# Loads, splits and sums of x placed sooner, one weight sum placed inside the first block pair, and q's raw weights issued ahead of the last transpose

## The chip, the cores and the metric

The kernel runs on one core of one Trainium2 chip. The core has a matrix engine (PE, TensorE), which writes its results to the PSUM memory, three engines for element-wise work (DVE or VectorE, ACT or ScalarE, POOL or GpSimd) and a queue engine (SP) that issues most DMA transfers. Each engine works through its own instructions strictly in order and waits at each one for the semaphores that this instruction needs. The metric is the device time of one execution in microseconds (us), as the median of several runs.

## The reference

One input x (2048 rows of 512) goes through two mixers, and a sigmoid gate blends them:

```python
x = A_x
g = _sigmoid((x * gate_w).sum(-1, keepdims=True))
a = _A_ref(x, A_wqkv, A_w_phi, A_wo)
b = _B_ref(x, B_w_q, B_k1, B_k2, B_u, B_v)
return g * a + (1 - g) * b
```

`_A_ref` is linear attention with 32 heads of 16: q, k and v are projections of x; q and k go through a small matrix per head and then a pair of softmaxes, softmax(p) and softmax(-p); `kv` is the sum over all rows of phi_k times v, and the output is phi_q times kv over a normalising sum, times `wo`. `_B_ref` picks for each row and head one of 16 x 16 experts by two maxima over scores (x times `w_q` times the keys `k1`, `k2`), and adds up rows of `v` weighted by a gelu of x times `u`.

## The kernel before

**Blocks.** x is worked on in 16 blocks of 128 rows. The first phase (up to about 157 us) builds what has to be there before any output row: k and v of all 16 blocks and their sum kv, and the folded score weights. The main stage after it computes one output block after the other.

**Three-product matmuls.** Every float32 operand is split into a high part (names ending in h, a copy rounded to the fp32r type) and a low part (ending in l, the difference to the original). A product is then three matmuls, high x high, high x low and low x high (`mm3`, L56 to L58, and `prod`, L446). So each block of x needs a load (`x_load`, L149, SP), a high copy `xh` (`x_high`, L152, on ACT from block 3 on) and a low part `xl` (`x_low`, L156, on DVE). The loaded blocks share four buffers `xr`.

**Blocks 0 to 4** are done singly, in the loop over t. A block has its projections `vproj` and `kproj` on PE, `k_diffs` on DVE (two reductions L115 and L117 and two subtractions L119 and L121: the differences to maximum and minimum, for the two softmaxes), `k_exp` on ACT (L266), `k_sum` on DVE (L270 and the reciprocal L271), `k_mult` on POOL (L275), and later `kvacc` on PE (L282), which adds phi_k times v to kv.

**Blocks 5 to 14** are done in five pairs, t = 5, 7, 9, 11, 13, by a scheme that saves products: seven half-size products instead of eight, with sums of the pair's two blocks (`Sums.add`, four POOL additions in place on the two `xr` buffers, L175 to L178; then `Sums.high` gives `gh` and a second high part on ACT, L183, and `Sums.low` gives `gl` and a second low part on POOL, L188) and with sums of the weights (t1, t2, e and t4, each in a high and a low part; t2h and t2l lie in `uh` and `ul`, and the fourth, t4h and t4l, in a part of `sh` and `sl`). The partial results a, b, c and d (banks named pk, pu, pv, pk) build upon each other: ACT copies a to b (L474), b to c (L483) and b to d (L502) between the products. In the order of PE a pair is: pk (6 matmuls), pe (6), pu (6), pk (6), two score sums `ws`, kvacc, pu (6), pv (6), pk (6).

**Score weights.** The raw weights `w_q` come in 16 pieces of 1 MB (`load_wq`, two buffers `st`, also used for wv, wk and q's raw weights `rawq`). `score` (L298) folds one piece into the bank `ws`. After each second piece `score_planes` (L303, L305) splits the result into two planes of 16 bits on ACT and transposes them by a DMA on SP; `score_join` puts the planes together again (L310, ACT), makes the high part `sh` (L314, ACT) and the low part `sl` (L315, POOL). The planes `wpl`, the transposed planes `wtp` and the joined `wtj` have one buffer each, so the eight rounds follow one another. A new `load_wq` is issued as soon as a score piece has been used.

**The end of the phase.** After the last pair come block 15 alone, the fold of q's weights (`fold_q`, L207, needs `rawq`), the first rows of the scores `front_s(0, 0)` and `front_s(0, 1)` (banks s; the second needs all of joins 4 to 7), the remaining kvacc, and `front_q(0)` (bank pq).

**What sets the order.** The schedule is manual: each engine's instructions stand in the order in which the Python code calls them. Moving a call moves its instruction on every engine that it uses. SP's queue is in order too, so that a load whose buffer is not yet free holds up all that stand behind it.

Of the kernel before, what the change touches and what calls it, by code (L numbers as in the profile page):

```python
# [9 lines left out]
F32 = mybir.dt.float32  # L10
# [6 lines left out]
ALU = mybir.AluOpType  # L17
# [3 lines left out]
P = 128  # L21
S = 2048
D = 512
NT = S // P
# [11 lines left out]
def mix_kernel(ctx, tc, xT, wqT, wkT, wv, wphi, wo, wq, kk, ug, ev, cst, out):  # L36
    nc = tc.nc
    pe, dve, act, pool, sp = nc.tensor, nc.vector, nc.scalar, nc.gpsimd, nc.sync
# [4 lines left out]
    def mm_bank(name):  # L43
        return psum.tile([P, 512], F32, tag="mm", bufs=4, name=name)

    def tr_bank(name):
        return psum.tile([P, 512], F32, tag="tr", bufs=3, name=name)
# [44 lines left out]
    t1h = per.tile([P, 2, D], F32R, name="t1h")  # L92
    t1l = per.tile([P, 2, D], F32R, name="t1l")
# [39 lines left out]
    wa_ = ca.enter_context(tc_pool("wl", "left"))  # L133
# [6 lines left out]
    def stage(src, name, shape=None):  # L140
        t_ = wa_.tile(shape or [P, NK, D], F32, tag="st", bufs=2, name=name)
        if src is not None:
            sp.dma_start(t_, src)
        return t_

    def x_load(t):
        r = rawx[t] = wa_.tile([P, NK, P], F32, tag="xr", bufs=4, name=f"xr{t}")
        if t > 0:
            sp.dma_start(r, xT[t])  # L149

    def x_high(t, ks=slice(0, NK)):
        (dve.tensor_copy if t < 3 else act.copy)(x_of(t)[0][:, ks], rawx[t][:, ks])  # L152

    def x_low(t, ks=slice(0, NK)):
        h, l = x_of(t)
        dve.tensor_tensor(l[:, ks], rawx[t][:, ks], h[:, ks], op=ALU.subtract)  # L156

    def x_split(t, ks=slice(0, NK)):
        x_high(t, ks)
        x_low(t, ks)  # L160

    kraw, t12 = (m.rearrange("p (k d) -> p k d", k=NK) for m in raw4)
    t1r, t2r = t12[:, 0:2], t12[:, 2:4]
    twos = lambda a: a.rearrange("p k n -> p (k n)")[:, :1024].rearrange("p (k n) -> p k n", k=2)
    t2h, t2l = twos(uh), twos(ul)
    t4h, t4l = sh[:, :, 768:1024], sl[:, :, 768:1024]
# [73 lines left out]
    phis, vs, pks, wsP, stk, joins = {}, {}, {}, {}, {}, []  # L240
# [20 lines left out]
    def kproj(t):  # L261
        pks[t] = mm_bank(f"pk{t}")
        proj(pks[t], t, wah, wal, 0, D)

    def k_exp(t):
        act.activation(phis[t], phis[t], AF.Exp)  # L266

    def k_sum(t):
        d, st = phis[t], stk[t]
        dve.tensor_reduce(st[:, 64:128], g64(d), axis=AX.X, op=ALU.add)  # L270
        dve.reciprocal(st[:, 128:192], st[:, 64:128])  # L271

    def k_mult(t):
        d, st = phis[t], stk.pop(t)
        pool.tensor_tensor(g64(d), g64(d), b64(st[:, 128:192]), op=ALU.mult)  # L275
# [17 lines left out]
    def score_w(i, raw):  # L293
        j, par = i // 2, i % 2
        if par == 0:
            wsP[j] = tr_bank(f"ws{j}")
        for c in range(4):
            pe.matmul(wsP[j][32 * c:32 * c + 32, :], kp[:, j // 4, par, :], raw[:, c, :],  # L298
                      start=(par == 0), stop=(par == 1))
# [7 lines left out]

    def score_join(j, tp):
        tj = wa_.tile([P, D], F32, tag="wtj", bufs=1, name=f"wtj{j}")
        act.copy(tj.bitcast(U16).rearrange("p (k n j) -> p j k n", j=2, n=P),  # L310
                 tp.rearrange("p (j k) n -> p j k n", j=2))
        js = slice(P * j, P * j + P)
        t3 = tj.rearrange("p (k e) -> p k e", k=NK)
        act.copy(sh[:, :, js], t3)  # L314
        pool.tensor_tensor(sl[:, :, js], t3, sh[:, :, js], op=ALU.subtract)  # L315
# [22 lines left out]
    x_load(1)  # L338
    rawk = stage(wkT, "rawk")
    x_load(2)  # L340
    wps = mm_bank("warm")
    for _ in range(16):
        pe.matmul(wps[:, :384], warm[:, 1:P + 1], warm[:, :384], start=True, stop=True)
# [27 lines left out]
    def load_wq():  # L371
        if len(raws) < 16:
            raws.append(stage(wq[len(raws)], f"wq{len(raws)}"))

    load_wq()
    load_wq()
    pool.tensor_copy(wm, cs[:, 128:160].rearrange("p (a b) -> p a b", b=F))

    pool.tensor_tensor(t1r, t1r, kraw[:, 0:2], op=ALU.subtract)
    pool.tensor_tensor(t2r, t2r, kraw[:, 0:2], op=ALU.add)  # L380
    act.copy(t1h, t1r)
    pool.tensor_tensor(t1l, t1r, t1h, op=ALU.subtract)

    def spare(src, name, shape):
        t_ = wa_.tile(shape, F32, tag="xr", bufs=4, name=name)
# [5 lines left out]
    def score(n):  # L391
        nonlocal done
        for _ in range(n):
            score_w(done, raws[done])
            done += 1
            load_wq()
            if done % 2 == 0:
                score_planes(done // 2 - 1)

    def join_all():  # L400
        old = list(joins)
        joins.clear()
        for j, tp in old:
            score_join(j, tp)

    plan = {0: 2, 2: 1, 3: 1, 4: 2}
    for t in range(5):
        x_load(t + 3)
        if t > 2:
            vproj(t)()  # L410
        kproj(t)
        k_diffs(t)
        score_old = list(joins)
        joins.clear()
        score(plan.get(t, 0))
        if t % 2 == 0:
            for u in (t - 3, t - 2):
                if u >= 0:
                    kvacc(u)
        if t > 0:  # L420
            x_split(t + 2)
        k_exp(t)
        k_sum(t)
        if t == 0:
            act.copy(t2h, t2r)
            pool.tensor_tensor(t2l, t2r, t2h, op=ALU.subtract)
        k_mult(t)
        if t == 2:
            t4r = kraw[:, 2:4]
            pool.tensor_tensor(t4r, t4r, t2r, op=ALU.subtract)  # L430
            by4 = lambda a: a.rearrange("p k (c n) -> p (k c) n", c=2)
            act.copy(t4h, by4(t4r))
        for j, tp in score_old:
            score_join(j, tp)
    x_load(8)
    Sums.add(5)
    Sums.high(5)
    Sums.low(5)
    pool.tensor_tensor(t4l, by4(t4r), t4h, op=ALU.subtract)
    x_high(7)  # L440
    x_high(8)

    def prod(o, left, right, first):
        for i, ((ah, al), (bh, bl)) in enumerate(zip(left, right)):
            for j, (x_, w_) in enumerate(((ah, bh), (ah, bl), (al, bh))):
                pe.matmul(o, x_, w_, start=(first and i + j == 0), stop=(i == 1 and j == 2),  # L446
                          skip_group_check=True)
# [8 lines left out]
    for t in range(5, NT - 1, 2):  # L456
        n = t + 1
        more = [u for u in (t + 4, t + 5) if u < NT]
        for u in more:
            x_load(u)  # L460
        if t == NT - 5:
            rawu = [spare(ug[:, 0:2], "rawu0", [P, 2, NU])]
        elif t == NT - 3:
            rawu.append(spare(ug[:, 2:4], "rawu1", [P, 2, NU]))
            rawe = [spare(ev[:, 0], "rawe0", [P, D])]
        for u in (t + 2, t + 3):
            if u < NT - 1:
                x_low(u)
        if behind:
            k_diffs(behind)  # L470
        a = pks[t] = mm_bank(f"pk{t}")
        prod(a, tile_of(t, 0), b11, True)
        b = mm_bank(f"pu{t}")
        act.copy(b, a)  # L474
        if t + 3 < NT:
            Sums.add(t + 2)
        if t < NT - 3:
            join_all()
        e = tr_bank(f"pe{t}")
        prod(e, sums(0, 2), b1, True)  # L480
        prod(b, sums(1, 0), b2, False)
        c = mm_bank(f"pv{t}")
        act.copy(c, b)  # L483
        prod(a, tile_of(t, 2), b21, False)
        k_diffs(t)
        if behind:
            k_exp(behind)
            k_sum(behind)
            k_mult(behind)
        score(2)  # L490
        if t == NT - 3:
            rawq = stage(wqT, "rawq")
        for u in (t - 3, t - 2):
            if u > 2:
                kvacc(u)
        k_exp(t)
        k_sum(t)
        vn, vt = v_tile(n), v_tile(t)
        act.copy(vn, by16(e))
        prod(b, sums(0, 0), b3, False)  # L500
        d = pks[n] = mm_bank(f"pk{n}")
        act.copy(d, b)  # L502
        prod(c, sums(1, 2), b22, False)
        dve.tensor_tensor(vt, by16(c), vn, op=ALU.add)
        dve.tensor_tensor(vn, by16(b), vn, op=ALU.add)
        o2 = d.rearrange("p (c n) -> p c n", c=2)
        prod(o2, tile_of(n, 2), b4, False)
        if t + 3 < NT:
            Sums.high(t + 2)
            Sums.low(t + 2)  # L510
        if t == 7:
            for i in range(2):
                x_parts(i, 11)
        for u in more if n < NT - 4 else ():
            x_high(u)
        k_mult(t)
        behind = n
    t = NT - 1
    x_split(t)
    rawe.append(spare(ev[:, 1], "rawe1", [P, D]))  # L520
    k_diffs(t - 1)
    kproj(t)
    k_exp(t - 1)
    k_sum(t - 1)
    for k in range(NK):
        act.copy(uh[:, k, :NU], rawu[k // 2][:, k % 2, :])
        pool.tensor_tensor(ul[:, k, :NU], rawu[k // 2][:, k % 2, :], uh[:, k, :NU], op=ALU.subtract)
    k_mult(t - 1)
    k_diffs(t)
    join_all()  # L530
# [357 lines left out]
    for a in range(NT - 1):  # L888
        n, b, z = a + 1, a - 1, a - 2
# [74 lines left out]
    a, b, z = NT - 1, NT - 2, NT - 3  # L964
# [123 lines left out]
```

## Time and profile before

| | |
|---|---|
| median of 3 runs | 408.52 us (408.52 to 409.42) |
| time of the profiled execution | 410.26 us |
| its span | 407.8 us |
| mean granted TensorE clock | 0.958 |
| busy, share of the span | PE 92%, DVE 81%, ACT 62%, POOL 50% |
| chain that ended last, by engine | PE 73%, DVE 9%, ACT 7%, POOL 4% |
| DMA | 46.67 MB, mean 114 GB/s |

A timeline row gives the start, the length, the engine, the line, the operation with out<-in, the shapes and the count, and in brackets how long the engine was idle before it and which instruction ended that. "PEq" and "SPq" are the queues' own instructions, such as a DMA that is issued. A row of a window gives busy time of PE, PEld, DVE, ACT and POOL, then the granted clock of TensorE (1.00 is full speed), the share of the DMA engines and GB/s. PE's matmuls overlap, so one that is listed with 0.39 us starts 0.23 us after the one before it at full clock.

### The profile page before, as it was taken

The numbers are of one execution on the slowest core, as the hardware profiler recorded it, in microseconds if no ns is written. First come the engines' busy times: TensorE is split into PE (matmuls) and PEld (weight loads), VectorE is DVE, ScalarE is ACT, GpSimd is POOL, SyncE is SP. The second block draws the span as 40 slices with busy tenths as digits, with TensorE's granted clock in tenths as the row PEclk, the third lists the DMA queues.
The fourth block names the chain that finished last, engine by engine and source line by source line (L and its number), as shares of the span: only waits on it lengthen the run. The fifth ranks groups of instructions, "written<-read, shape, count | busy, mean of one in ns | idle before, by whom it ended". The sixth has DMA issues, their size and how long they took to land.

```text
span 407.8 us, 8985 instructions
## 1 busy us (share of the span) xinstructions
PE 375.5 (92%) x3519; PEld 294.2 (72%) x3519; DVE 331.9 (81%) x782; ACT 253.1 (62%) x449; POOL 202.4 (50%) x206
## 2 busy tenths in 40 slices
PE   8998909999998099989999999999999999999996
PEld 4756605776776088868878888888888888888775
DVE  4679536898969409687999999999999999999993
ACT  4564544677743603558769669668677877877731
POOL 1095469777963621448326335444543633554700
PEclk9998966999999669998999999999999999999999
DMA  7755582989670501133542344235145135324111
GB/s 277 260 217 196 166 248 61 276 220 268 132 237 2 155 2 32 50 78 92 79 91 73 72 90 92 66 80 104 26 105 116 39 80 116 61 71 105 39 54 51
DMA packets 72218, 46.67 MB, mean 114 GB/s; under 512 B 63600, under 2 KB 64496, under 8 KB 69872
## 3 DMA queue, kind: packets, MB, share of 16 engines
q1 hardware_dynamic: 71312, 45.24, 42.2%
q10 hardware_dynamic: 864, 0.87, 0.8%
q8 instruction: 27, 0.44, 0.5%
q14 instruction: 15, 0.12, 0.1%
HBM read 26.43 MB, written 4.19 MB: 75 GB/s over the span
## 4 chain that ended last, share of the span: by engine, by line
PE 73%; DVE 9%; ACT 7%; POOL 4%; issue 3%; DMA 3%; SPq 0%; ACTq 0%; POOLq 0%; DVEq 0%
PE po L817 10%; PE s L56 8%; PE s L57 7%; PE s L58 7%; PE po L824 5%; PE pq L56 4%; PE pq L58 4%; PE pq L57 4%; PE pk L446 3%; PE oT L708 2%; PE pu L446 2%; DVE xl L156 2%; PE pp L57 2%; PE pp L58 2%; PE pp L56 2%
## 5 line engine op out<-in xcount | busy, mean ns | idle before, releaser
L622 POOL TENSOR_TENSOR w<-d,zb 128x512 f32<-128x512 f32 x32 | 40.9, 1294 | 83.5 <-ACT d L616 83.5
L56 PE MATMUL s<-sh,xh 128*128 128x512 f32 x128 | 52.3, 408 | 0.0
L57 PE MATMUL s<-sl,xh 128*128 128x512 f32 x128 | 51.1, 399 | 0.0
L58 PE MATMUL s<-sh,xl 128*128 128x512 f32 x128 | 51.0, 398 | 0.0
L275 POOL TENSOR_TENSOR d<-d,st 128x1024 f32<-128x1024 f32 x16 | 32.3, 2020 | 37.2 <-DVE st L271 25.2
L657 POOL TENSOR_TENSOR d<-d,st 128x512 f32<-128x512 f32 x30 | 31.2, 1062 | 28.5 <-DVE st L651 25.6
L616 ACT ACTIVATE d<-d 128x512 f32<-128x512 f32 x32 | 20.1, 632 | 39.8 <-DVE d L119 31.1
L699 ACT COPY pt<-tp 128x1024 uint16<-128x1024 uint16 x28 | 36.4, 1370 | 0.0
L156 DVE TENSOR_TENSOR xl<-xr,xh 128x512 fp32r<-128x512 f32 (+2 forms) x17 | 23.2, 1380 | 12.4 <-ACT xh L152 12.3
L689 ACT COPY pl<-d 128x1024 uint16<-128x1024 uint16 x28 | 29.2, 1045 | 4.3 <-POOL d L657 4.3
L58 PEld LDWEIGHTS s<-sh,xl 128*128 128x128 f32 x128 | 24.7, 193 | 5.3
L56 PEld LDWEIGHTS s<-sh,xh 128*128 128x128 f32 x128 | 24.8, 194 | 5.0
L57 PEld LDWEIGHTS s<-sl,xh 128*128 128x128 f32 x128 | 24.8, 194 | 4.8
L56 PE MATMUL pq<-wah,xh 128*128 128x512 f32 x64 | 26.8, 418 | 0.0
L626 DVE TENSOR_REDUCE st<-d 128x32 f32<-128x512 f32 x32 | 21.7, 682 | 5.4 <-ACT d L616 3.8
L58 PE MATMUL pq<-wah,xl 128*128 128x512 f32 x64 | 25.1, 392 | 0.0
L57 PE MATMUL pq<-wal,xh 128*128 128x512 f32 x64 | 25.0, 390 | 0.0
L266 ACT ACTIVATE d<-d 128x1024 f32<-128x1024 f32 x16 | 17.0, 1062 | 12.2 <-DVE d L121 12.2
L270 DVE TENSOR_REDUCE st<-d 128x64 f32<-128x1024 f32 x16 | 19.3, 1205 | 6.4 <-ACT d L266 6.3
L817 PE MATMUL po<-wbh,xh 128*128 128x512 f32 x60 | 24.0, 400 | 0.0
L817 PE MATMUL po<-wbl,xh 128*128 128x512 f32 x60 | 23.4, 390 | 0.0
L666 DVE TENSOR_TENSOR eq<-s,mx 128x512 bf16<-128x512 f32 x32 | 22.1, 692 | 1.2
(240 smaller groups left out, 1113.6 us busy)
## 6 DMA issues: line engine op xcount, KB each, us to landing
wq<-wq SPq DMA_DIRECT2D x16, 1024.0 KB, 6.0
xr<-xT SPq DMA_DIRECT2D x15, 256.0 KB, 4.7
y<-ot SPq DMA_DIRECT2D x15, 256.0 KB, 2.5
rawk<-wkT SPq DMA_DIRECT2D x1, 1024.0 KB, 6.7
rawq<-wqT SPq DMA_DIRECT2D x1, 1024.0 KB, 4.9
rawo<-wo SPq DMA_DIRECT2D x4, 256.0 KB, 3.6
rawu<-ug SPq DMA_DIRECT2D x2, 258.0 KB, 3.5
rawv<-wv ACTq DMA_DIRECT2D x2, 256.0 KB, 4.7
```

Of the source, the lines that this page charges most:

```text
L56: pe.matmul(o, ah, bh, start=(first and i == 0), stop=False)
L57: pe.matmul(o, ah, bl, start=False, stop=False)
L58: pe.matmul(o, al, bh, start=False, stop=(last and i == n - 1))
L156: dve.tensor_tensor(l[:, ks], rawx[t][:, ks], h[:, ks], op=ALU.subtract)
L275: pool.tensor_tensor(g64(d), g64(d), b64(st[:, 128:192]), op=ALU.mult)
L622: pool.tensor_tensor(hs(e["w"], i), hs(e["ph"], i), hs(zb, i), op=ALU.mult)
L626: dve.tensor_reduce(pair(e["st"][:, 64:128])[:, :, i], hs(e["ph"], i), axis=AX.X, op=ALU.add)
L657: eng.tensor_tensor(g64(d)[:, gs_], g64(d)[:, gs_], r[:, gs_].unsqueeze(2).to_broadcast([P, 32, F]), op=ALU.mult)
L666: dve.tensor_tensor(e["eq"][:, 512 * half:512 * half + 512].rearrange("p (h f) -> p h f", f=F), p3, mx.unsqueeze(2).to_broadcast([P, H, F] ...
L689: act.copy(pl, e["ph"][:, halves[i]].bitcast(U16).rearrange("p (c j) -> p j c", j=2))
L699: act.copy(p16[:, :, 4 * i:4 * i + 4, :], e["tp"][i].rearrange("p (j g) n -> p j g n", j=2))
L817: pe.matmul(po, a, b, start=(i == 0), stop=False)
```

## The change

It moves calls and changes no arithmetic:

- x3 is loaded before the warm-up, x4 to x6 before the first block, x7 and x8 in blocks 1 and 2; before, block t loaded x(t + 3), and x8 came after the loop. Splits go one block ahead: block t < 3 splits x(t + 3), and block 2 also x6.
- The first sums (`Sums.add(5)`, high, low) go from behind the loop into blocks 2 and 3.
- The low part t1l goes into block 0, the difference t4r from block 2 to block 3, and its parts t4h and t4l into pair 5. `k_mult(4)` goes into pair 5, behind t4l.
- The first joins come in blocks 2 and 4 (before: 1 and 4), each before that block's score sum.
- `score_join` is cut in two, `join_tp` (the copy that empties `wtp`) and `join_end`. In pair 13 the seventh join's first half is done; its second half follows behind the pair.
- In pair 13 `rawq` is issued between the two score sums, and x15 is split inside the pair. Behind the pair the parts of u come ahead of `k_exp(14)`.

```diff
@@ score_join
     def score_join(j, tp):
         tj = wa_.tile([P, D], F32, tag="wtj", bufs=1, name=f"wtj{j}")
+        join_tp(j, tp, tj)
+        join_end(j, tj)
+
+    def join_tp(j, tp, tj):
         act.copy(tj.bitcast(U16).rearrange("p (k n j) -> p j k n", j=2, n=P),
                  tp.rearrange("p (j k) n -> p j k n", j=2))
+
+    def join_end(j, tj):
         js = slice(P * j, P * j + P)
         t3 = tj.rearrange("p (k e) -> p k e", k=NK)
         act.copy(sh[:, :, js], t3)
...
     x_load(2)
+    x_load(3)
...
     load_wq()
     load_wq()
+    for t in (4, 5, 6):
+        x_load(t)
...
     act.copy(t1h, t1r)
-    pool.tensor_tensor(t1l, t1r, t1h, op=ALU.subtract)
...
-    plan = {0: 2, 2: 1, 3: 1, 4: 2}
+    t4r = kraw[:, 2:4]
+    by4 = lambda a: a.rearrange("p k (c n) -> p (k c) n", c=2)
     for t in range(5):
-        x_load(t + 3)
+        if t in (1, 2):
+            x_load(t + 6)
         if t > 2:
             vproj(t)()
         kproj(t)
         k_diffs(t)
-        score_old = list(joins)
-        joins.clear()
-        score(plan.get(t, 0))
+        if t in (2, 4):
+            join_all()
+        score((2, 0, 1, 1, 2)[t])
         if t % 2 == 0:
             for u in (t - 3, t - 2):
                 if u >= 0:
                     kvacc(u)
-        if t > 0:
-            x_split(t + 2)
+        if t < 3:
+            x_split(t + 3)
+        if t == 2:
+            x_split(6)
+            Sums.add(5)
+        if t == 3:
+            Sums.high(5)
+            Sums.low(5)
         k_exp(t)
         k_sum(t)
         if t == 0:
             act.copy(t2h, t2r)
+            pool.tensor_tensor(t1l, t1r, t1h, op=ALU.subtract)
+        if t < 4:
+            k_mult(t)
+        if t == 0:
             pool.tensor_tensor(t2l, t2r, t2h, op=ALU.subtract)
-        k_mult(t)
-        if t == 2:
-            t4r = kraw[:, 2:4]
+        if t == 3:
             pool.tensor_tensor(t4r, t4r, t2r, op=ALU.subtract)
-            by4 = lambda a: a.rearrange("p k (c n) -> p (k c) n", c=2)
-            act.copy(t4h, by4(t4r))
-        for j, tp in score_old:
-            score_join(j, tp)
-    x_load(8)
-    Sums.add(5)
-    Sums.high(5)
-    Sums.low(5)
-    pool.tensor_tensor(t4l, by4(t4r), t4h, op=ALU.subtract)
     x_high(7)
     x_high(8)
...
+        if t == 5:
+            act.copy(t4h, by4(t4r))
         if t < NT - 3:
             join_all()
+        else:
+            (j6, tp), = joins
+            joins.clear()
+            tj6 = wa_.tile([P, D], F32, tag="wtj", bufs=1, name="wtj6")
+            join_tp(j6, tp, tj6)
+        if t == 5:
+            pool.tensor_tensor(t4l, by4(t4r), t4h, op=ALU.subtract)
+            k_mult(4)
...
-        score(2)
+        score(1)
         if t == NT - 3:
             rawq = stage(wqT, "rawq")
+        score(1)
...
         prod(c, sums(1, 2), b22, False)
+        if t == NT - 3:
+            x_split(NT - 1)
         dve.tensor_tensor(vt, by16(c), vn, op=ALU.add)
...
     t = NT - 1
-    x_split(t)
     rawe.append(spare(ev[:, 1], "rawe1", [P, D]))
     k_diffs(t - 1)
     kproj(t)
-    k_exp(t - 1)
-    k_sum(t - 1)
+    join_end(j6, tj6)
     for k in range(NK):
         act.copy(uh[:, k, :NU], rawu[k // 2][:, k % 2, :])
         pool.tensor_tensor(ul[:, k, :NU], rawu[k // 2][:, k % 2, :], uh[:, k, :NU], op=ALU.subtract)
+    k_exp(t - 1)
+    k_sum(t - 1)
     k_mult(t - 1)
```

POOL from the end of block 2 to the first sums, before (L275 is `k_mult`, L430 the difference t4r, L245 sets a column of v, L315 a join's low part, L175 to L178 the adds):

```order
L275 TENSOR_TENSOR d_374<-d_374,st_375 128x1024
L430 TENSOR_TENSOR xraw_66<-xraw_66,xraw_69 128x1024
L245 MEMSET v_442 128x32
L275 TENSOR_TENSOR d_458<-d_458,st_459 128x1024
L245 MEMSET v_495 128x32
L275 TENSOR_TENSOR d_511<-d_511,st_512 128x1024
L315 TENSOR_TENSOR sl<-wtj_604,sh 128x4x128
L175 TENSOR_TENSOR xr_427<-xr_427 128x256
L176 TENSOR_TENSOR xr_427<-xr_359,xr_427 128x256
L177 TENSOR_TENSOR xr_359<-xr_427,xr_359 128x256
L178 TENSOR_TENSOR xr_359<-xr_359 128x256
L188 TENSOR_TENSOR gl<-xr_427,gh 128x512
```

And now, from the second `k_mult` (L321 is the join's low part, L448 the difference t4r):

```order
L275 TENSOR_TENSOR d_351<-d_351,st_352 128x1024
L321 TENSOR_TENSOR sl<-wtj_384,sh 128x4x128
L175 TENSOR_TENSOR xr_285<-xr_285 128x256
L176 TENSOR_TENSOR xr_285<-xr_283,xr_285 128x256
L177 TENSOR_TENSOR xr_283<-xr_285,xr_283 128x256
L178 TENSOR_TENSOR xr_283<-xr_283 128x256
L275 TENSOR_TENSOR d_378<-d_378,st_379 128x1024
L245 MEMSET v_452 128x32
L188 TENSOR_TENSOR gl<-xr_285,gh 128x512
L188 TENSOR_TENSOR xl_70<-xr_283,xh_67 128x512
L275 TENSOR_TENSOR d_468<-d_468,st_469 128x1024
L448 TENSOR_TENSOR xraw_66<-xraw_66,xraw_69 128x1024
```

The adds stood behind five `k_mult`; now they stand behind two, and `gl` behind three.

ACT in pair 5, between the copies to b and c, before (L474 and L483 are these copies, L310 and L314 the third join):

```order
L152 CAST xh_65<-xr_608 128x512
L474 COPY pu_634<-pk_627 128x512
L310 COPY wtj_640<-wtp_532 128x2x512
L314 CAST sh<-wtj_640 128x4x128
L483 COPY pv_657<-pu_634 128x512
```

And now (L483 and L502 are the copies, L487 is t4h, L314 and L320 the third join):

```order
L152 CAST xh_65<-xr_363 128x512
L483 COPY pu_631<-pk_624 128x512
L487 CAST sh<-xraw_66 128x4x256
L314 COPY wtj_638<-wtp_547 128x2x512
L320 CAST sh<-wtj_638 128x4x128
L502 COPY pv_657<-pu_631 128x512
```

t4h has come between the two copies; the join was there before and still is.

SP at the end of the phase, before (L305 is the transpose of the last planes, L143 the load of `rawq`):

```order
L143 DMA wq_1186<-wq 128x2048
L305 DMA_TRANSPOSE wtp_1190<-wpl_1188 128x8x128
L386 DMA rawu_1291<-ug 128x516
L386 DMA rawe_1293<-ev 128x512
L305 DMA_TRANSPOSE wtp_1352<-wpl_1350 128x8x128
L143 DMA rawq<-wqT 128x2048
```

And now:

```order
L143 DMA wq_1186<-wq 128x2048
L305 DMA_TRANSPOSE wtp_1190<-wpl_1188 128x8x128
L394 DMA rawu_1291<-ug 128x516
L394 DMA rawe_1293<-ev 128x512
L143 DMA rawq<-wqT 128x2048
L305 DMA_TRANSPOSE wtp_1356<-wpl_1354 128x8x128
```

`rawq` has moved ahead of the last transpose, which waits for its `wtp` buffer.

## The prediction

> **What bounds the kernel now.** I read the list of who waited for whom on PE over the whole span first, since page part 2 shows PE at 9 tenths nearly everywhere; columns are total us, times, longest.
>
> ```profile
> PE foldq L207 <- DMA rawq<-wqT: 10.1, 1, 10.1
> PE pe L446 <- ACT gh L183: 9.6, 1, 9.6
> ...
> PE kvacc L282 <- POOL d L275: 1.8, 1, 1.8
> PE pk L58 <- DVE xl L156: 1.3, 1, 1.3
> ```
>
> Two waits of some 10 us each stand out: pair 5 for the first sums, and the fold of q for its raw weights. The windows say what else they cost: busy time of PE, PEld, DVE, ACT, POOL, then the granted clock.
>
> ```profile
> 30.00:40.00 10.00, 8.21 (x96) 6.20 (x88) 9.93 (x11) 4.63 (x5) 5.38 (x4) 0.83 0.63 212
> 60.00:70.00 10.00, 7.94 (x30) 5.23 (x34) 5.39 (x4) 5.23 (x8) 9.06 (x9) 0.63 0.17 53
> 120.00:130.00 10.00, 8.75 (x170) 5.94 (x168) 8.69 (x12) 4.82 (x7) 3.95 (x4) 1.00 0.01 3
> 140.00:150.00 10.00, 7.39 (x74) 6.55 (x75) 0.00 (x0) 2.60 (x4) 3.73 (x3) 0.53 0.26 107
> 340.00:350.00 10.00, 10.00 (x87) 8.17 (x86) 9.59 (x25) 7.12 (x12) 3.99 (x4) 1.00 0.42 96
> ```
>
> Behind each wait PE runs slowly (0.63 and 0.53), then at 1.00 with PE full to the end. So what PE gains before 157 us arrives at the end whole, and all else is free until PE waits for it.
>
> **First gap: the sums of blocks 5 and 6.** PE's last matmul ahead of it, POOL's first add and what follows the adds, and PE's first matmul of the next pair, in order of time:
>
> ```profile
> 51.09 0.40 PE L446 MATMUL pk<-wah,xl 128*128 128x512 f32 x1
> 58.85 0.72 POOL L175 TENSOR_TENSOR xr<-xr 128x256 f32<-128x256 f32 x1
> 61.94 1.29 POOL L188 TENSOR_TENSOR gl<-xr,gh 128x512 fp32r<-128x512 f32 x1
> 75.66 0.39 PE L446 MATMUL pk<-wah,xh 128*128 128x512 f32 x1
> ```
>
> The four adds of the sums stand on POOL behind the fifth k_mult and a join's low part, run from 58.85 to 61.94, and pair 5 ends only at 75.66.
>
> PE's own order does not change, so I replay what PE needs. Two kinds of rows give the lengths: the chain of waits for PE, and the timeline of the first blocks for DVE.
>
> ```profile
> 104.14 1.36 PE pe L446 x6
> ...
> 108.22 1.85 PE ws L298 x16
> ```
>
> ```profile
> 25.56 2.40 POOL L382 TENSOR_TENSOR t1l<-xraw,t1h 128x1024 fp32r<-128x1024 f32 x1
> 30.27 1.92 POOL L275 TENSOR_TENSOR d<-d,st 128x1024 f32<-128x1024 f32 x1
> 30.28 2.46 DVE L156 TENSOR_TENSOR xl<-xr,xh 128x512 fp32r<-128x512 f32 x1
> 48.50 1.22 DVE L270 TENSOR_REDUCE st<-d 128x64 f32<-128x1024 f32 x1 [0.26 <-ACT d L266]
> 50.23 0.63 DVE L115 TENSOR_REDUCE st<-pk 128x32 f32<-128x512 f32 x1
> 51.96 0.68 DVE L121 TENSOR_TENSOR d<-st,pk 128x512 f32<-128x512 f32 x1
> 52.56 0.69 DVE L156 TENSOR_TENSOR xl<-xr,xh 128x512 fp32r<-128x512 f32 x1
> ```
>
> A block's differences take 2.4 us (50.23 to the end of L121), its sum and reciprocal 1.75 (48.50 to 50.23). The low part xl takes 0.69 alone; beside a POOL operation it took 2.46, ending 0.55 after POOL did. The Trainium skill, "SBUF — State Buffer", section "SBUF: two separate sides", says that of a VectorE operation with two SBUF inputs and a GpSimd one the first to start keeps a shared port for its whole length; the 2.46 agrees.
>
> The loads of x3 to x6, now ahead of the first block, cost SP four issues of some 0.4 us in a stretch where it idles. They also move 0.75 MB more ahead of about 20 us; bound 0 to 2 us of delay for the second weight load, against 21.8 us where PE wants it. I take 0. On SP the load of x8 now waits for DVE's xl4 (35.2 below), and the next weight load stands behind it:
>
> ```profile
> wq<-wq SPq DMA_DIRECT2D x16, 1024.0 KB, 6.0
> ```
>
> Issued at 35.3 instead of 30.5 it lands near 41.5; PE wants it at 46.9, so the late transfer is hidden, with 5 us to spare. Without that cover each microsecond more would cost PE one.
>
> POOL's t1l, t2l and the later t4r are moved behind more urgent work but not lengthened. DVE then runs: xl3 to 28.5 (behind POOL's t1l), sum 30.25, differences of block 1 to 32.65, xl4 35.2 (behind t2l), sum 36.95, differences of 2 to 39.35, xl5 40.8 (behind sl), xl6 41.5. So the four adds run on POOL from 41.5 to 44.65 instead of 58.85 to 61.94. k_mult of block 0 stays at 30.3, hence PE's 1.8 us wait and its slow stretch stay too. POOL goes on with k_mult(2) to 46.6, gl to 48.05, xl, k_mult(3) to 51.25, t4r to 53.65. PE wants gh and gl only from 51.2: the wait goes.
>
> What is late next is ACT. It does exp(4) when DVE ends block 4's differences (50.95), then the two high parts of x7 and x8, then copies pu at 53.2 to 53.8. PE, done with pe (51.2 + 1.36 = 52.55), waits **1.25 us** for that. It goes pu 55.15, pk 56.5, score 58.35, kvacc 59.1, and then needs ACT's copy pv, which stands behind the third join, and that join behind its transposed planes. The transposes land behind the two weight loads issued just before them:
>
> ```profile
> 48.98 0.89 SPq L143 DMA_DIRECT2D wq<-wq  x2
> 54.98 1.24 SPq L305 DMA_TRANSPOSE wtp<-wpl  x1
> 82.32 1.68 SPq L143 DMA_DIRECT2D wq<-wq  x2
> 84.45 2.34 SPq L305 DMA_TRANSPOSE wtp<-wpl  x1
> DMA to landing us min/median/max: 4.1/4.1/4.1
> DMA to landing us min/median/max: 10.2/10.2/10.2
> ```
>
> The last two lines are those two transposes: 54.98 + 4.1 is 10.1 after the first weight load, 84.45 + 10.2 is 12.3 after. With the first load now at 48.0 (half of the score that starts at 46.9 unchanged) I take 9.7, near the first of these: landing 57.7. The join (1.33, and 0.62 as every cast of that size, rows below) and the copy end at 60.2, so PE waits **1.1 us**; bound 0 to 3.7. Behind that copy on ACT stand the next planes, exp(5), v and the copy pk. Then pu 61.6, pv 62.95, **0.35** for ACT's copy pk (the fourth sum's low part t4l, now at the end of POOL's queue, is due at 63.2), pk 64.65. Pair 5 ends 11.0 us sooner. Pair 7 then wants gl when POOL, still busy with t4l and k_mult(4) to 65.1, has it at 66.5; PE would reach it at about 66: **0.5**. POOL and PE keep the same distance in later pairs as before, where POOL waits 2 us for DVE. **Term one: 10.5 us**, bounds 6.2 (all of the late landing) to 13.5 (no new wait).
>
> **Second gap: q's weights.**
>
> ```profile
> 126.74 0.62 ACT L152 CAST xh<-xr 128x512 fp32r<-128x512 f32 x1 [0.61 <-PE pv L446]
> 127.42 1.94 POOL L275 TENSOR_TENSOR d<-d,st 128x1024 f32<-128x1024 f32 x1
> 132.32 1.06 ACT L266 ACTIVATE d<-d 128x1024 f32<-128x1024 f32 x1 [4.96 <-DVE d L121]
> 134.50 1.33 ACT L310 COPY wtj<-wtp 128x1024 uint16<-128x1024 uint16 x1
> 137.63 0.33 SPq L143 DMA_DIRECT2D rawq<-wqT  x1
> 142.61 3.64 PE L207 MATMUL foldq<-wp,rawq 32*128 32x32 f32 x64 [10.09 <-DMA rawq<-wqT]
> 150.56 1.99 PE L207 MATMUL foldq<-wp,rawq 32*128 32x32 f32 x64
> 152.48 1.27 PE L282 MATMUL kvacc<-v,d 128*32 128x17 f32 x128
> 153.68 0.50 PE L56 MATMUL s<-sh,xh 128*128 128x512 f32 x1
> 156.63 0.74 PE L282 MATMUL kvacc<-v,d 128*32 128x17 f32 x64
> 157.30 0.51 PE L56 MATMUL pq<-wah,xh 128*128 128x512 f32 x1
> ```
>
> Now rawq stands on SP behind the transposes of the last planes, these wait for the one wtp buffer, and ACT empties it (L310) only at 134.5. Changed, SP issues rawq after the 15th weight sum, at 121.9 of the old clock (half of the score that the old run begins at 121), and even at 5 us to land it is there at 127, before PE wants it. From 132.5 (142.61 less 10.1) PE then does foldq 1.92, s 2.95, foldq 1.92, kvacc 1.2, s 2.95, kvacc 0.7 (differences of the starts from 150.56 on) = 11.6 us, where the old run took 24.8 to reach pq at 157.30. **Term two: 13.2 us.**
>
> Its cover: the second s needs the last join's low part on POOL. From the block differences that chain is 2.4 + 1.06 + 1.75 + k_mult 1.94 + 1.29 (as gl) = 8.4 us, from 131.2 (xl at 129.9, then the two v additions) to 139.6, while s comes at 140.4: 0.8 us to spare. The seventh join's first half, moved into pair 13, puts 1.33 us ahead of ACT's copy pv; PE reads that copy 4 us later, so nothing.
>
> xl of block 15 is moved ahead of DVE's two v additions. The old 1.3 us wait goes if DVE takes it at 127.4, and stays if POOL's k_mult, starting at 127.42, comes first; xh ends at 127.36. Bounds 0 and 1.3; with 0.06 us between them I take half, **0.6**. By the port rule of the Trainium skill's page "SBUF — State Buffer", section "SBUF: two separate sides", it is the one or the other and nothing between: 384.8 or 383.5 us.
>
> **Sum.** 10.5 + 13.2 + 0.6 = 24.3 us. The profiled execution took 410.26 with a span of 407.8, so 386.0 with a span of 383.5; the median is 408.52, 1.74 lower, so **384.2**.
>
> **Rivals.** *The join takes the gap's place.* The transposes land 12.3 us after the load: PE waits 3.7 instead of 1.1 and its clock falls. For: the 1.8 us wait left 0.83 in the window 30 to 40, that is 1.7 us, while 1.3 us in 120 to 130 left 1.00. Against: only one of the landings was that slow. 2.6 + 1.7 = 4.3: 388.5.
>
> *The tail gets a new wait.* The 0.8 us of cover is small; if POOL has the last low part 2.3 us later, s waits 1.5 and the clock 1.7 more: 387.4.
>
> *The first part does not do what it says.* If each of xl3 to xl6 loses one more POOL operation of 2.4 us, the adds start near 51, gl is at 57.7, and PE waits 6.4 us and slowly returns (the old return cost 3.9 beyond its wait). Term one falls to about 2: 392.7. Against: the old order shows one POOL operation lost per xl, not two.
>
> *Slower: the clock of the main stage.* With the rests gone PE is full from 32 us on. If that made the granted clock sag over the 250 us after 157, the sum is eaten at 0.91 (250 x 0.1 = 25); at the 0.83 seen above it would be 51 us, 435. Against: PE at 10.00 busy holds 1.00 in 340 to 350.
>
> **How the numbers follow.** Forecast 0.65 (381.5 to 387), join 0.14, tail 0.08, first part idle 0.07, clock 0.05, and 0.01 for no change. The range goes from 380.5 (no new waits, 1.3 in full) to 391.5 (join and tail together). Within 0.3% is what this kernel's measurement cannot tell from none: faster 0.94, same 0.01, slower 0.05.
>
> **What would show it.** Right: gh and rawq gone from PE's waits; the adds on POOL near 41 us; pair 7 starting near 64.7; waits of about 1 us for pu and pv; rawq issued near 111; pq starting near 133; 1.00 in every window after. Wrong: PE waiting over 2 us for pv or for the last low part, or a clock below 0.95 in the main stage.

## The result, and the profile after

The changed kernel takes 384.60 us in the median of four runs (383.04 to 386.55), against 408.52 us before: a ratio of 0.941, with a 95% interval of 0.937 to 0.946. The forecast was 384.2 us. Its profiled execution took 383.04 us with a span of 381.3 us, 26.5 us less than the 407.8 before. PE is now busy for 96% of the span (92% before).

Who waited for whom on PE, changed kernel (total us, times, longest):

```profile
PE pu L455 <- ACT pu L483: 2.0, 1, 2.0
PE kvacc L282 <- ACT v L254: 2.0, 1, 2.0
PE kvacc L282 <- POOL d L275: 1.9, 1, 1.9
...
```

Both long waits, the one for `gh` and the one for `rawq`, are gone, and nothing above 2.0 us has taken their place. The windows of the changed kernel, same columns as before the change:

```profile
30.00:40.00 10.00, 8.09 (x105) 5.39 (x98) 9.96 (x13) 4.58 (x6) 7.09 (x4) 1.00 0.59 186
60.00:70.00 10.00, 9.07 (x37) 6.47 (x36) 8.33 (x10) 7.07 (x12) 10.00 (x9) 1.00 0.79 247
140.00:150.00 10.00, 10.00 (x52) 8.51 (x51) 8.19 (x25) 5.20 (x13) 5.33 (x5) 1.00 0.12 28
340.00:350.00 10.00, 10.00 (x53) 8.13 (x52) 9.55 (x26) 7.39 (x12) 4.47 (x6) 1.00 0.49 107
```

Before, the granted clock stood at 0.83, 0.63 and 0.53 in the first three of these; now it is 1.00 in all of them (the window 140 to 150 holds later work than it did before). In this execution the main stage, 340 to 350, stayed at 1.00 too.

The first gap, in the timeline of the changed kernel (start, length, engine, line, operation; in brackets the idle time before it and what ended it):

```profile
39.30 2.23 DVE L156 TENSOR_TENSOR xl<-xr,xh 128x512 fp32r<-128x512 f32 x2
41.61 0.74 POOL L175 TENSOR_TENSOR xr<-xr 128x256 f32<-128x256 f32 x1 [1.23 <-DVE xl L156]
46.64 1.19 SPq L143 DMA_DIRECT2D wq<-wq  x2
49.97 0.39 PE L455 MATMUL pe<-t1h,gh 128*128 128x512 f32 x1
52.86 0.57 ACT L483 COPY pu<-pk 128x512 f32<-128x512 f32 x1
53.49 0.50 PE L455 MATMUL pu<-uh,xh 128*128 128x512 f32 x1 [1.99 <-ACT pu L483]
56.41 1.37 ACT L314 COPY wtj<-wtp 128x1024 uint16<-128x1024 uint16 x1 [1.85 <-DMA wtp<-wpl]
58.34 0.58 ACT L502 COPY pv<-pu 128x512 f32<-128x512 f32 x1
58.97 0.50 PE L455 MATMUL pu<-eh,gh 128*128 128x512 f32 x1
62.84 0.50 PE L455 MATMUL pk<-sl,xh 128*128 128x512 f32 x1 [0.51 <-POOL sl L496]
64.09 0.39 PE L455 MATMUL pk<-wah,xh 128*128 128x512 f32 x1
66.43 0.50 PE L455 MATMUL pe<-t1h,gl 128*128 128x512 f32 x1 [0.36 <-POOL gl L188]
```

The adds start on POOL at 41.61 instead of 58.85, as soon as DVE has the low parts of x5 and x6, and pair 7 begins at 64.09 instead of 75.66. The second gap, same columns:

```profile
110.42 0.33 SPq L143 DMA_DIRECT2D rawq<-wqT  x1
...
115.82 2.50 POOL L275 TENSOR_TENSOR d<-d,st 128x1024 f32<-128x1024 f32 x1
115.83 0.69 DVE L156 TENSOR_TENSOR xl<-xr,xh 128x512 fp32r<-128x512 f32 x1 [0.49 <-ACT xh L152]
119.33 1.99 PE L207 MATMUL foldq<-wp,rawq 32*128 32x32 f32 x64
130.92 0.51 PE L56 MATMUL pq<-wah,xh 128*128 128x512 f32 x1
```

`rawq` is issued at 110.42, the fold of q runs without a wait, and pq starts at 130.92 instead of 157.30. Behind pq nothing changed: to the end of the span it is 250.4 us, and was 250.5.

### The profile page after: what moved, and what is told of

It reads as the page before. It is cut to its first block, busy times and chain, and to the rows that moved or that the text cites. A ratio compares the mean times of both kernels' runs of the same rounds, so it can differ in the third digit from the quotient of the medians.

```text
span 381.3 us, 8988 instructions
## 1 busy us (share of the span) xinstructions
PE 367.1 (96%) x3519; PEld 287.5 (75%) x3519; DVE 330.0 (87%) x782; ACT 253.0 (66%) x449; POOL 204.0 (53%) x206
## 4 chain that ended last, share of the span: by engine, by line
PE 76%; POOL 7%; DVE 5%; ACT 4%; DMA 4%; issue 3%; ACTq 0%; POOLq 0%
PE po L839 11%; PE s L56 7%; PE s L57 7%; PE s L58 7%; PE po L846 5%; PE pq L56 5%; PE pq L58 4%; PE pq L57 4%; PE pk L455 3%; PE oT L730 3%; DMA wtp<-wpl 2%; PE pp L57 2%; PE pp L58 2%; PE pp L56 2%; PE pu L455 2%
## 5 line engine op out<-in xcount | busy, mean ns | idle before, releaser
L56 PE MATMUL s<-sh,xh 128*128 128x512 f32 x128 | 51.0, 399 | 0.0
L57 PE MATMUL s<-sl,xh 128*128 128x512 f32 x128 | 49.9, 390 | 0.0
L58 PE MATMUL s<-sh,xl 128*128 128x512 f32 x128 | 49.9, 390 | 0.0
L275 POOL TENSOR_TENSOR d<-d,st 128x1024 f32<-128x1024 f32 x16 | 32.5, 2030 | 17.7 <-ACT v L519 7.8
L56 PEld LDWEIGHTS s<-sh,xh 128*128 128x128 f32 x128 | 24.0, 188 | 4.7
L156 DVE TENSOR_TENSOR xl<-xr,xh 128x512 fp32r<-128x512 f32 (+2 forms) x17 | 21.1, 1261 | 2.0 <-ACT xh L152 1.9
```

Of the source, the lines that this page charges most:

```text
L56: pe.matmul(o, ah, bh, start=(first and i == 0), stop=False)
L57: pe.matmul(o, ah, bl, start=False, stop=False)
L58: pe.matmul(o, al, bh, start=False, stop=(last and i == n - 1))
```

## The experiments

Theory: two stalls of PE were removed, one by the sums placed sooner, the other by `rawq` and the seventh join. PE was full between and behind them, so the gains add up, and what is left of 1 to 2 us waits is passed on from one ACT copy to the next. The rivals differ by experiment. Ratios are against the kernel before, timed beside each kernel on the same chip. It took 408.52 us beside the changed kernel and 409.49 to 409.80 us beside the others, so ratios compare better across the rows than medians do.

| kernel | median us | ratio, 95% interval | start of pair 7 | start of pq |
|---|---|---|---|---|
| changed | 384.60 | 0.941, 0.937 to 0.946 | 64.09 | 130.92 |
| first part alone | 399.44 | 0.976, 0.972 to 0.980 | 64.25 | 145.84 |
| end part alone | 395.08 | 0.963, 0.961 to 0.966 | 75.83 | 142.55 |
| `rawq` alone | 398.78 | 0.973, 0.970 to 0.976 | 75.74 | 145.74 |
| join alone | 396.94 | 0.968, 0.965 to 0.971 | 76.36 | 143.99 |
| sums late | 389.88 | 0.952, 0.948 to 0.957 | 70.34 | 136.93 |
| x15 behind | 386.13 | 0.942, 0.938 to 0.947 | 63.74 | 131.77 |
| pair 5 reordered | 383.37 | 0.936, 0.933 to 0.939 | 63.69 | 131.00 |
| v15 sooner | 383.00 | 0.934, 0.930 to 0.939 | 64.29 | 131.15 |
| block 0 into kv later | 383.29 | 0.936, 0.934 to 0.938 | 65.35 | 131.30 |
| pair 5 and v15 | 382.76 | 0.935, 0.933 to 0.938 | 62.93 | 130.05 |
| all three | 381.33 | 0.931, 0.929 to 0.934 | 62.15 | 129.93 |

The starts are each from one profiled execution, and the medians of the last six rows also carry the spread of four runs (the changed kernel's own is 3.5 us).

**First part alone** (the changed kernel without its end part):

```diff
 in pair t = 13
-            join_tp(j6, tp, tj6)
-        score(1)
+        score(2)
         if t == NT - 3:
             rawq = stage(wqT, "rawq")
-        score(1)
...
-            x_split(NT - 1)
 behind the pair
+    x_split(t)
...
```

> The change without its end: loads, splits, sums, fourth weight sum and first joins as changed; q's raw weights, the seventh join, the split of x15 and the order of exp(14) as before. Theory (two separate gaps, each filled by its own part): 408.5 less 11.6, about 397, the wait for rawq still 10 us. Rival (both parts fill one and the same slack, so one alone gives nearly all): below 390. Rival (the first gap is only handed on to the end): above 404.

PE's waits in it:

```profile
PE foldq L207 <- DMA rawq<-wqT: 9.8, 1, 9.8
...
PE pk L58 <- DVE xl L156: 1.2, 1, 1.2
```

399.44 against 409.63 us, 10.2 less, where the theory had 11.6; by the traces pq starts 11.46 us sooner than before (145.84 against 157.30). Both end waits stand as they stood before within 0.3 us, and the first gap is closed: pair 7 starts at 64.25. Neither rival's time came.

**End part alone** (the kernel before, with the other half of the diff: `rawq`, the seventh join's two halves, x15 and the parts of u).

> The kernel before with the end of the change alone. Theory: 408.5 less 13.2 to 14.8, so 394 to 395, the wait for gh still 9.6 us. Rival (one common slack): below 388 or above 402.

From its waits and its window 30 to 40:

```profile
PE pe L452 <- ACT gh L183: 9.6, 1, 9.6
...
30.00:40.00 10.00, 8.16 (x96) 6.20 (x88) 9.93 (x11) 4.62 (x5) 5.46 (x4) 0.83 0.62 213
```

395.08 against 409.63 us, 14.55 less, while the first gap keeps its 9.6 us. The product of the two ratios, 0.9757 x 0.9634 = 0.940, is the changed kernel's 0.941: the parts add up, and neither needs the other.

**`rawq` alone and the join alone** (two edits to the kernel before; which of them closes the second gap?):

```diff
 rawq alone
-        score(2)
+        score(1)
         if t == NT - 3:
             rawq = stage(wqT, "rawq")
+        score(1)
```

```diff
 join alone
...
+        else:
+            (j6, tp), = joins
+            joins.clear()
+            tj6 = wa_.tile([P, D], F32, tag="wtj", bufs=1, name="wtj6")
+            join_tp(j6, tp, tj6)
...
     k_exp(t - 1)
     k_sum(t - 1)
+    join_end(j6, tj6)
```

> The kernel before, with q's raw weights issued between the last two score sums and nothing else moved. Theory: rawq lands near 127, the fold starts at 132.5 at once, but the last transpose is as late as before, so the second half of the first scores waits 2 to 3 us for the last join's low part: 397.5 to 399.5. Rival (the place of rawq on the queue is all): 395. Rival (the joins bound, rawq was only last in line): above 403.

> The kernel before, with only the seventh join cut in two and its first half in the last pair; rawq still behind the last transpose. Theory (the one wtp buffer held up the transpose and with it rawq): the transpose goes near 124, rawq near 125.5, landing near 130.5 before PE wants it at 132.5: 395.3, as much as the whole end. Rival (rawq must be moved past the transpose): above 402.

The timeline of `rawq` alone: SP's two issues, ACT's copy out of `wtp`, and PE.

```profile
121.40 0.33 SPq L143 DMA_DIRECT2D rawq<-wqT  x1
135.28 1.24 SPq L305 DMA_TRANSPOSE wtp<-wpl  x1
133.89 1.36 ACT L310 COPY wtj<-wtp 128x1024 uint16<-128x1024 uint16 x1
140.98 0.49 PE L56 MATMUL s<-sh,xh 128*128 128x512 f32 x1 [1.05 <-ACT sh L314]
142.33 0.50 PE L57 MATMUL s<-sl,xh 128*128 128x512 f32 x1 [0.85 <-POOL sl L315]
```

The timeline of the join alone:

```profile
119.72 1.36 ACT L314 COPY wtj<-wtp 128x1024 uint16<-128x1024 uint16 x1 [2.67 <-DMA wtp<-wpl]
123.48 2.04 SPq L305 DMA_TRANSPOSE wtp<-wpl  x1
126.05 0.33 SPq L143 DMA_DIRECT2D rawq<-wqT  x1
132.04 1.99 PE L207 MATMUL foldq<-wp,rawq 32*128 32x32 f32 x64
```

With `rawq` alone the load no longer waits, but the last transpose still does, until ACT has emptied `wtp` at 135.25; so the last join is late and the second s waits twice, 1.05 and 0.85 us. With the join alone ACT empties `wtp` at 121.1, the transpose follows at 123.48 and `rawq` at 126.05, and the fold waits for nothing. So the late emptying of the one `wtp` buffer held up the transpose, and with it the load behind it; a second `wtp` buffer was not tried. Alone the two edits save 10.85 and 12.7 us, and the end part that holds both, and x15 besides, 14.55: they remove the same stall, and their gains must not be added. `rawq` alone came out as its theory said. The join alone is 1.6 us above the 395.3 that its theory gave for the whole end: its pq starts 1.44 us later than that of the end part, and a wait of 1.23 us for the low part of x15 still stands in it at 129.52, which the end part does not have.

**Sums late** (the changed kernel with the sums' calls behind the loop again; is it their place in the order, and not the sooner loads, that closes the first gap?):

```diff
-            Sums.add(5)
-        if t == 3:
-            Sums.high(5)
-            Sums.low(5)
...
+    Sums.add(5)
+    Sums.high(5)
+    Sums.low(5)
     x_high(7)
```

> The changed kernel with its early loads and splits, but the first sums (adds, high and low parts) called behind the loop again. Theory (their place in POOL's and ACT's order is what removed the first gap): the adds start behind the third k_mult, t4r and a join's low part near 54.5, gh is at 56.6 and gl near 59, PE waits 6 to 8 us for them and returns slowly: 391 to 394. Rival (the late load of x6 was the cause): 385.

From its waits, its timeline and its windows:

```profile
PE pe L454 <- ACT gh L183: 6.3, 1, 6.3
...
48.12 1.94 POOL L275 TENSOR_TENSOR d<-d,st 128x1024 f32<-128x1024 f32 x1 [3.23 <-PE kvacc L282]
53.60 0.71 POOL L175 TENSOR_TENSOR xr<-xr 128x256 f32<-128x256 f32 x1
...
50.00:60.00 10.00, 3.20 (x7) 2.10 (x8) 4.11 (x5) 4.92 (x8) 8.97 (x10) 0.59 0.65 167
```

389.88 us, between the theory's 391 to 394 and the rival's 385: neither holds alone. The adds run at 53.60, 12.0 us later than in the changed kernel, and `gh` is waited for 6.3 us, with the clock at 0.59 behind it. Pair 7 starts 6.25 us later than in the changed kernel (70.34 against 64.09), of the 11.6 that the first part gained. The place of the sums' calls is therefore about half of the first part. The rest must lie in the other moves, since even here the adds are 5.25 us sooner than before. POOL's timeline of the kernel before shows where on POOL these 5.25 us arise (the last two `k_mult` ahead of the adds):

```profile
50.48 1.94 POOL L275 TENSOR_TENSOR d<-d,st 128x1024 f32<-128x1024 f32 x1 [5.87 <-DVE st L271]
55.74 1.93 POOL L275 TENSOR_TENSOR d<-d,st 128x1024 f32<-128x1024 f32 x1 [3.23 <-ACT sh L314]
```

With the sums late `k_mult(3)` starts 2.36 us sooner (48.12 against 50.48). The other 2.9 us lie between it and the adds: there `k_mult(4)` stood with an idle time of 3.23 us ahead of it, and now the difference t4r stands there. No run takes these moves apart.

**x15 behind** (the changed kernel with x15 split behind the pair again):

```diff
-        if t == NT - 3:
-            x_split(NT - 1)
...
+    x_split(t)
```

> The changed kernel with the split of x15 behind the last pair again. Theory: PE's wait of 1.2 us for that low part is back and nothing covers it: 1.3 us more than the change, about 386. Rival (the place makes no difference, POOL's k_mult holds DVE up either way): 384.6.

Its timeline and its window 150 to 160, which has the 2.0 us wait for v15 in it:

```profile
117.69 0.50 PE L58 MATMUL pk<-wah,xl 128*128 128x512 f32 x1 [1.23 <-DVE xl L156]
...
150.00:160.00 10.00, 8.02 (x98) 6.28 (x97) 9.55 (x23) 5.99 (x11) 4.79 (x4) 0.85 0.33 65
```

The 1.2 us wait is back. From the start of pair 7 to that of pq it is 68.03 us, against 66.83 in the changed kernel, so the wait costs its 1.2 us in the trace. The time, 386.13 us, is 1.5 above the changed kernel's, but the ratios (0.942 and 0.941) lie inside each other's intervals; so the times neither show the cost nor speak against it.

**Pair 5 reordered** (what is the 2.0 us wait for ACT's copy pu worth?). On ACT the copy to pu comes first, then the high parts of x7 and x8 and exp(4), then the copy to pv; t4h and the third join come behind both. On POOL t4l comes ahead of the second sums and `k_mult(4)` behind them:

```diff
-        k_exp(t)
-        k_sum(t)
+        if t < 4:
+            k_exp(t)
+            k_sum(t)
...
+            x_high(7)
+            x_high(8)
+            k_exp(4)
+            x_low(7)
+            x_low(8)
+            k_sum(4)
...
```

> The changed kernel with pair 5 reordered: on ACT the copies to pu and pv come ahead of exp(4) and of the third join, the high parts of x7 and x8 stand between; on POOL t4l comes ahead of the second sums and k_mult(4) behind them. Theory (ACT's order makes the new waits of 2.0 and 0.5 us, and POOL's order the next pair's): up to 3.5 us less, 381. Rival (POOL's sum of work binds, the wait only moves to gl of pair 7): 384.6.

From its waits and its timeline of DVE:

```profile
PE pk L454 <- ACT pk L529: 2.5, 2, 1.9
...
51.60 4.44 DVE L156 TENSOR_TENSOR xl<-xr,xh 128x512 fp32r<-128x512 f32 x2 [0.47 <-ACT xh L152]
59.41 0.68 DVE L121 TENSOR_TENSOR d<-st,pk 128x512 f32<-128x512 f32 x1
```

The wait for pu is gone, and PE waits 1.9 us for the copy pk instead. That copy stands on ACT behind exp(5), exp(5) needs DVE's differences (done at 60.1), and these now stand behind two low parts that took 4.44 us. Pair 7 starts 0.4 us sooner, and pq does not (131.00 against 130.92). The wait moved, though not to gl of pair 7 as the rival had it, and the theory's 381 us was not reached.

**v15 sooner** (the 2.0 us wait of kvacc for v15, which stood in both kernels; v15 is copied ahead of the second block's exponentials, the last copy of kv ahead of the join):

```diff
-        soft_exp(a)
         if a == 1:
             v15()
...
+        soft_exp(a)
...
```

> The changed kernel with v of block 15 copied ahead of the second block's exponentials on ACT, and the final copy of kv ahead of the join behind it. Theory (PE waits 2.0 us for that copy in both kernels, behind DVE's subtractions): 382 to 383. Rival (DVE binds that stage, so the wait goes elsewhere): 384.6.

The two places in its list of PE's waits:

```profile
PE po L839 <- ACT xh L734: 1.7, 1, 1.7
...
PE oT L730 <- ACT pt L721: 0.7, 1, 0.7
```

The wait for v15 is gone, and two new ones of 1.7 and 0.7 us stand behind it. The median, 383.00 us, lies in the theory's 382 to 383, but the span of the profiled execution was 381.1 us against 381.3: the trace shows the rival's moved wait, and no gain of 1.6 us.

**Block 0 into kv later** (is the 1.9 us wait for the first `k_mult` worth its length?):

```diff
+        if t == 3:
+            kvacc(0)
...
-                if u >= 0:
+                if u >= 1 or (u == 0 and t != 2):
```

> The changed kernel, with block 0's 64 matmuls into kv moved from behind block 2's projection to behind block 3's. Theory A (the wait before that work is only passed on, because the instruction that PE meets next, pair 5's first product of the second sums, waits for ACT's copy pu at a fixed time): kvacc's wait of 1.9 us on POOL goes, the pu wait grows from 2.0 to about 3.9, the start of pair 7 stays within 0.5 us of 64.1, and the time is 384.6, 383 to 386. Rival B (the wait is worth its length): the pu wait stays 2.0, pair 7 starts near 62.2, the time is about 382.7. Rival C (a wait of nearly 4 us drops the clock, which one of 2 us did not): the window 60 to 70 shows a granted clock under 0.9 and the time is 386 or more.

From its waits and its timeline:

```profile
PE pu L457 <- ACT pu L485: 3.1, 1, 3.1
...
PE kvacc L282 <- POOL d L275: 0.5, 1, 0.5
...
53.10 0.80 PE L457 MATMUL pu<-uh,xh 128*128 128x512 f32 x1 [3.07 <-ACT pu L485]
53.69 0.63 PE L457 MATMUL pu<-ul,xh 128*128 128x512 f32 x1
```

The wait for `k_mult` fell by 1.4 us, and the wait for pu grew by 1.1. The products behind it took 0.63 us instead of 0.39 (a clock of 0.66 in the window 50 to 60), and pair 7 began 1.26 us later than in the changed kernel. So theory A holds for the most part: a wait was passed on. Its start of pair 7 was missed by 0.8 us, for the clock of rival C, which came in the window 50 to 60 and not in 60 to 70. The time, 383.29 us, is not above the changed kernel's, so rival C's price did not show, and rival B's gain is not in the trace (pq at 131.30, against 130.92).

**Combinations.** Pair 5 and v15 together, and with block 0 into kv later too:

> The changed kernel with the two later edits of the experiments together: pair 5 reordered on ACT and POOL, and block 15's copy of v ahead of the second block's exponentials with the last copy of kv ahead of the join. Theory: each edit left a new wait behind it of nearly the old length (ACT's copy pk 1.9, the second block's high part 1.7), so the sum of both is what each gave alone against the changed kernel's 384.6: 1.2 and 1.6, so 381.8, range 380.5 to 383.5. Rival (both single gains were run to run spread of the clock): 384.6, 383.5 to 386.

> As the combination of pair 5's reordering and block 15's copy of v, and with block 0's 64 matmuls into kv behind block 3's projection too. With pair 5 reordered the pu wait is gone, so that PE reaches that pair 1.9 us sooner and meets ACT's copies there. Theory A (ACT and DVE set that pair's end, PE's lead is lost in the copies): the wait for the copy pk or pu grows from 1.9 to about 3.8, the time is that of the combination without this edit, within 0.7 us. Rival B (PE's lead is kept): 1.5 to 2 us less than that combination, near 380.

The window 60 to 70 of the first, behind a wait of 1.8 us for the copy pk:

```profile
60.00:70.00 10.00, 8.42 (x42) 5.89 (x46) 8.08 (x9) 8.35 (x13) 8.80 (x8) 1.00 0.49 162
```

And of the second, behind the same wait of 1.8 us:

```profile
60.00:70.00 10.00, 9.73 (x42) 7.12 (x46) 8.44 (x11) 7.36 (x12) 9.99 (x9) 0.83 0.37 116
```

The first is at 382.76 us, inside its expectation. It is only 0.6 and 0.2 us below the two edits alone, so that their gains add up is not shown. In the second PE got past the copy pk 1.2 us sooner (60.27 against 61.44), the wait for it did not grow to 3.8, and so theory A was wrong on its place; but the clock fell, and at pq the lead was 0.1 us (129.93 against 130.05). The medians differ by 1.4 us, more than theory A's 0.7 and just short of rival B's 1.5 to 2, and the two spans by 0.3; which of the two is the edit's worth stays open. All three together, at 381.33 us, are the fastest kernel of this study; its interval (0.929 to 0.934) lies below the changed kernel's (0.937 to 0.946), though the two were not timed beside each other. The medians say 3.3 us and the profiled spans 1.5 (379.8 against 381.3). The spans compare the fastest of four executions of the changed kernel with the second slowest of all three together, so the true gain may well be above 1.5; three waits of together 5.9 us were attacked for it.

## Why the prediction was right

**The ledger of the span**, which closes. Predicted and measured, in us saved: to the start of pair 7, 11.0 and 11.57; the new wait for gl, -0.5 and -0.36; x15, 0.6 and 1.3; from the fold of q to pq, 13.2 and 13.19 (24.78 - 11.59); a wait that I had not listed, 0 and 0.8. Together 24.3 and 26.5, and the span fell by 26.5. The unlisted wait stands in the timeline of before:

```profile
101.13 0.50 PE L446 MATMUL pk<-sh,xh 128*128 128x512 f32 x1 [0.79 <-ACT pk L502]
```

It is pair 9's last product, waiting for ACT's copy pk. In the changed kernel no wait of PE between pair 7 and the fold is longer than 0.36 us. My replay stopped at pair 7 and took the later pairs as they were. (The five terms come to 0.1 more than pq's own move, 26.38 us, because a wait of 0.17 us at 89.54 is new.)

**The hit of 0.4 us is partly luck.** The profiled executions differ by 410.26 - 383.04 = 27.2 us, and I had 24.3, so 2.9 too little. I then took 1.74 off, because the profiled execution of before lay that far above its median. That of the changed kernel lay 1.56 below its own. The forecast was sound to about 3 us, not to 0.4.

**Term one, step by step.** The adds were to start at 41.5; they did at 41.61. DVE's replay held too: xl5 and xl6 were to end at 41.5, and ended at 41.53. What was mis-sized is PE's arrival. I had kept the slow stretch of clock (0.83) behind the 1.9 us wait for `k_mult`; in this execution the clock stayed at 1.00, and PE began pe, which needs `gh`, at 49.97 instead of 51.2. Most of that went into the next wait: pu took 1.99 instead of 1.25. The weight load, too, went out at 46.64 instead of 48.0; its transpose landed at 56.41, 9.8 us after it, where I had 9.7. So the join was done in time for ACT to copy pv from 58.34 to 58.92, just as PE's kvacc ended: no wait, where I had 1.1. t4l cost 0.51 (I had 0.35 for ACT's copy pk at the same place).

**Was the kept clock worth anything?** `rawq` alone answers it: there the clock in the window 30 to 40 was 1.00 too, with the first gap left as it was. Its wait for `gh` is 11.5 us instead of 9.6, and pair 7 starts at 75.74 instead of 75.66. In the old order the sooner arrival was lost whole in the gap; in the new one, pair 7 starts 0.56 us ahead of the prediction's 64.65, about half of the 1.2 us by which PE came sooner.

**Term two** was exact in size and right in its cause, which the two single edits show: one `wtp` buffer, emptied late, held up the transpose and the load queued behind it. The 0.8 us of cover for the last low part was enough.

**x15** was a draw between 0 and 1.3, and I took the half. By the trace DVE's low part began 0.01 us after POOL's `k_mult` (115.83 and 115.82), and it still took its usual 0.69 while `k_mult` took 2.50 instead of 1.94. In the end part alone DVE won in the same way (127.46 against 127.45), so the gain was the whole 1.3. That is the case for which the prediction gave 383.5 us; that the time came out nearer to the 384.8 of the other case is due to the other terms.

**The rivals.** The late join did not come (9.8 us, not 12.3, from load to landing). The tail's wait did not come. The first part did what it says. The clock of the main stage stayed at 1.00 in the profiled execution, and the slowest of the four, 386.55 us, leaves no room for the 25 us of that rival.

## What to carry to other kernels

Where one engine is full, look for the waits that break it and ask what stands ahead of the late thing in its queue: here calls placed sooner on POOL, ACT and SP were worth 26 us of a span of 408, with the same arithmetic. Two edits that undo the same hold-up, one by emptying the buffer sooner and one by taking the load out of the queue behind it, gain that stall once, so cost them together. Once the long waits are gone, the 2 us ones are held by the next copy in the same queue: removing one mostly names the next, and three such edits, aimed at 5.9 us of waits, gave 1.5 us of span and 3.3 us of median.

## What the runs showed of the hardware

**The clock behind a wait of 2 us is not fixed.** Behind the same wait of 1.8 to 1.9 us for `k_mult` near 30 us the granted clock of the window 30 to 40 was 0.83 in the kernel before and in the end part alone, and 1.00 in the other kernels that had this wait. The 2.0 us wait for v15 left 1.00 in the changed kernel and 0.85 where x15 was behind; 1.8 us for the copy pk left 1.00 and 0.83 in the two combinations. The wait of 1.2 us where x15 was behind left 1.00 (window 110 to 120), the one of 3.1 us for pu left 0.66, and those of 6 us and more in the windows quoted a low clock (0.53 to 0.63).

Where the clock fell, it fell for whole stretches. The end of one in the kernel before, in which PE's products come 0.43 us apart instead of 0.23:

```profile
36.22 0.60 PE L58 MATMUL pv<-wbh,xl 128*128 128x512 f32 x1
36.65 0.41 PE L56 MATMUL pv<-wbh,xh 128*128 128x512 f32 x1
```

It runs from 33.25 to 36.65 and another from 183.47 to 186.87, 3.4 us each; by these spacings one costs PE some 1.6 us of work (an estimate: 3.4 x (1 - 0.23 / 0.43)). The slow stretches of this execution end near 36.65, 67.35, 149.3 and 186.85 us, which lie 9, 24 and 11 times 3.41 us apart. Which wait starts such a stretch, and which does not, stays open.

The four runs of the changed kernel took 383.04, 384.31, 384.89 and 386.55 us at a mean clock of 1.000, 0.996, 0.994 and 0.987. That these drops fell behind its 2 us waits was not seen, since only the first was profiled. Nor is the clock all of the spread: with v15 sooner three runs at 0.999 took 381.42 to 383.14 us, and the slowest run of pair 5 and v15 together, 383.96 us, had 1.000.

The Trainium skill, "TensorE: Matmul & The Clock Gate", section "What's actually happening", says that the clock falls after an idle window of about 3.4 us, and that this window runs freely. The ends that lie whole multiples of 3.41 us apart agree with a free-running window; that the idle time must be 3.4 us does not agree, since waits of 1.8 us were enough in some executions here.

**The tie at the shared port went to the one that by the trace began 0.01 us later** (115.83 on DVE against 115.82 on POOL; 127.46 against 127.45 in the end part alone). The Trainium skill, "SBUF — State Buffer", section "SBUF: two separate sides", gives the port to the one that starts first; the starts of the trace do not resolve a difference of 0.01 us, and that one of the two ran at its usual length while the other was held for 0.56 us agrees with it.
